# Mixed attention and a SwiGLU feed-forward block on one core: a scheduled kernel rewritten with a hand-written order of 128-query tiles and 512-token groups

## The chip, the cores and the metric

The kernel runs on one core of one Trainium2 chip. The metric is device time in microseconds (us) of one execution; lower is better. A core has five engines that run beside each other, each working through its own queue in order: TensorE (PE in the profile; PEld is its loading of weights), VectorE (DVE), ScalarE (ACT), GpSimd (POOL) and SyncE (SP), which here issues all the DMA transfers. TensorE writes into PSUM, eight banks of 512 fp32 columns on 128 partitions.

## The reference, cut to what matters

Four batches, eight heads, 768 positions, head size 64. Heads 0, 2 and 6 ("retrieval") attend to all earlier positions; the other five ("streaming") attend to the first 4 positions (the sinks) and the last 64. The attention output, 3072 tokens by 512, goes through a SwiGLU feed-forward block of width 1536.

```python
    scores = scale * np.matmul(q, k.transpose(0, 1, 3, 2))
    causal = rel >= 0
    is_sink = pos[None, :] < int(n_sink)
    in_win = (rel >= 0) & (rel < int(window))
    stream_keep = causal & (is_sink | in_win)
    ...
    a = np.exp(scores)
    a = a / (np.sum(a, axis=-1, keepdims=True) + 1e-09)
    return np.matmul(a, v).astype(np.float32)

    g = x @ w_gate
    silu = g * (1.0 / (1.0 + np.exp(-g)))
    val = x @ w_val
    return (silu * val @ w_out).astype(np.float32)
```

## The kernel before

The program is written batch by batch, and a scheduler places its instructions in the engines' queues by priority, so that work of one batch can run among that of another where the queues and buffers allow it.

For a batch, q, k and v are loaded as six blocks of 128 positions each (lines 160, 161, 170; each transfer reads 256-byte runs), cast to half precision on ScalarE (q, line 162) and VectorE (k, line 163; v, line 173), and transposed on TensorE for two heads at a time (line 186), with the results copied out of PSUM by ScalarE (193) and VectorE (197).

Attention goes head by head over three blocks of 256 queries. Scores come transposed, keys on partitions: a matmul of 64 rows by 256 columns for each block of 128 keys (line 230), two blocks to a PSUM bank, then one exponential on ScalarE (235). A retrieval head takes all key blocks up to the queries' end, a streaming head takes three blocks, and its sinks are an extra matmul with 4 keys (210) and exponential (215). GpSimd multiplies the exponentials by a 0/1 mask (240). The value matmuls (249, and 255 for the sinks) take the exponentials as weights and 66 columns of v, one of them ones, so that the row's sum comes out beside the result; VectorE takes its reciprocal (261) and scales (264). When all heads of a batch are done, the six blocks are transposed once more (273) and copied into the feed-forward input xt (278).

The feed-forward block works on 256 tokens at a time: for each of 12 slices of 128 hidden units, four gate matmuls (291) and four value matmuls (296) of 256 columns into one PSUM bank, a tanh on ScalarE (301) and two products on VectorE (303, 308); then for each 128 tokens twelve output-projection matmuls of 512 columns (313), a copy by VectorE (318) and a store (319). The weights are loaded in large pieces through two staging buffers and cast on ScalarE and VectorE (lines 139, 141, 146), written after batch 0's attention.

What sets the order around the change is therefore the scheduler; nothing in the source says which attention instruction stands between which feed-forward matmuls.

## Time and profile before

| | |
|---|---|
| Median of 3 runs | 432.32 us (430.75 to 437.47) |
| Span of the profiled execution | 429.4 us (the page gives no other time of it) |
| TensorE busy | 377.4 us, 88%, 2760 matmuls |
| TensorE weight loads | 234.0 us, 55% |
| VectorE busy | 243.9 us, 57% |
| ScalarE busy | 190.9 us, 44% |
| GpSimd busy | 140.1 us, 33% |
| DMA | 35.06 MB, mean 82 GB/s |
| Granted TensorE clock, mean | 0.880 |

The profile is of one execution. Busy times are those in which an engine was at work on an instruction; matmuls are pipelined, so that the lengths of neighbours overlap and the distance between two starts says more about their cost than a length does. The page cuts the span into 40 slices and gives for each the busy share of each engine and the granted clock; the views below look into it by stretch, by group and by instruction.

### The profile page before, as it was taken

The numbers are of one execution on the slowest core, as the hardware profiler recorded it, in microseconds if no ns is written. First come the engines' busy times: TensorE is split into PE (matmuls) and PEld (weight loads), VectorE is DVE, ScalarE is ACT, GpSimd is POOL, SyncE is SP. The second block draws the span as 40 slices with busy tenths as digits, with TensorE's granted clock in tenths as the row PEclk, the third lists the DMA queues.
The fourth block names the chain that finished last, engine by engine and source line by source line (L and its number), as shares of the span: only waits on it lengthen the run. The fifth ranks groups of instructions, "written<-read, shape, count | busy, mean of one in ns | idle before, by whom it ended". The sixth has DMA issues, their size and how long they took to land.

```text
span 429.4 us, 7362 instructions
## 1 busy us (share of the span) xinstructions
PE 377.4 (88%) x2760; PEld 234.0 (55%) x2760; DVE 243.9 (57%) x754; ACT 190.9 (44%) x401; POOL 140.1 (33%) x117
## 2 busy tenths in 40 slices
PE   0578688999998989899999988899999988899995
PEld 0234334776674534676765543576766544576672
DVE  1253365687674373776765463586765543566763
ACT  3436848553245666233334765233334755122220
POOL 6145496001014676211003775410103786200000
PEclk9999999999999655699999755599999965599999
DMA  9991735977996471311010000000010000001001
GB/s 183 218 358 24 293 100 179 243 143 167 177 207 144 93 153 21 73 26 49 2 51 25 26 0 2 0 2 36 16 50 26 25 2 0 2 2 49 26 24 49
DMA packets 81090, 35.06 MB, mean 82 GB/s; under 512 B 75424, under 2 KB 75424, under 8 KB 81056
## 3 DMA queue, kind: packets, MB, share of 16 engines
q1 hardware_dynamic: 81056, 34.61, 33.6%
q8 instruction: 21, 0.34, 0.3%
q14 instruction: 13, 0.11, 0.1%
HBM read 28.31 MB, written 6.29 MB: 81 GB/s over the span
## 4 chain that ended last, share of the span: by engine, by line
PE 70%; ACT 9%; DVE 9%; issue 4%; POOL 4%; SPq 2%; DMA 1%; ACTq 0%; POOLq 0%
PE gv L291 15%; PE gv L296 13%; PE o_ps L313 13%; PE sc L230 11%; PE av L249 8%; ACT e L235 6%; POOL e L240 4%; PE trp L186 3%; PE xt_ps L273 2%; PE av L255 2%; ACT sig L301 2%; DVE sil L303 2%; DVE hj L308 2%; PE snk L210 2%; SPq L161 1%
## 5 line engine op out<-in xcount | busy, mean ns | idle before, releaser
L240 POOL TENSOR_TENSOR e<-e,cm 128x512 f16<-128x512 f16 (+1 forms) x96 | 132.9, 1391 | 227.1 <-ACT e L235 226.8
L301 ACT ACTIVATE sig<-gv 128x256 f32<-128x256 f32 x144 | 55.2, 383 | 147.1 <-PE gv L296 135.8
L235 ACT ACTIVATE e<-sc 128x512 f16<-128x512 f32 (+1 forms) x172 | 88.2, 546 | 64.0 <-PE sc L230 39.6
L291 PE MATMUL gv<-xt,wg_sb 128*128 128x256 f16 x576 | 91.0, 278 | 1.8 <-DVE hj L308 0.3
L296 PE MATMUL gv<-xt,wv_sb 128*128 128x256 f16 x576 | 90.6, 279 | 0.0
L230 PE MATMUL sc<-qt,ktt 64*128 64x256 f16 x304 | 79.5, 355 | 12.4 <-ACT e L235 10.5
L313 PE MATMUL o_ps<-wo_sb,hj 128*128 128x512 f16 x288 | 82.0, 380 | 1.7 <-DVE o_sb L318 0.8
L303 DVE SCALAR_TENSOR_TENSOR sil<-sig,gv 128x256 f32<-128x256 f32 x144 | 60.5, 420 | 38.9 <-ACT sig L301 38.6
L291 PEld LDWEIGHTS <-wg_sb 128*128 128x128 f16 x576 | 55.4, 100 | 22.4 <-issue 7.0
L249 PE MATMUL av<-vs,e 128*128 128x66 f16 x608 | 56.5, 229 | 11.1 <-POOL e L240 5.2
L249 PEld LDWEIGHTS <-e 128*128 128x128 f16 x608 | 38.0, 117 | 50.0 <-issue 21.2
L308 DVE TENSOR_TENSOR hj<-sil,gv 128x256 f16<-128x256 f32 x144 | 60.4, 420 | 4.7 <-PE o_ps L313 0.3
L296 PEld LDWEIGHTS <-wv_sb 128*128 128x128 f16 x576 | 57.4, 100 | 7.6
L261 DVE RECIPROCAL rc<-av 128x2 f32<-128x2 f32 x96 | 16.2, 169 | 78.4 <-PE av L255 41.4
L264 DVE TENSOR_SCALAR xb<-av,rc 128x64 f16<-128x64 f32 x192 | 45.5, 279 | 2.5
L230 PEld LDWEIGHTS <-ktt 64*128 64x128 f16 x304 | 25.2, 106 | 37.9 <-issue 25.2
L313 PEld LDWEIGHTS <-hj 128*128 128x128 f16 x288 | 27.7, 97 | 21.8 <-DVE hj L308 2.4
L318 DVE COPY o_sb<-o_ps 128x512 f32<-128x512 f32 x24 | 16.6, 692 | 27.6 <-PE o_ps L313 27.5
L273 PE MATMUL xt_ps<-identh,xb 128*128 128x128 f16 x96 | 19.2, 298 | 3.2 <-DVE xb L264 2.3
L255 PE MATMUL av<-vs,es 4*128 4x66 f16 x80 | 17.9, 224 | 0.0
L197 DVE COPY ktt<-trp 128x384 f16<-128x384 f16 x32 | 11.1, 354 | 11.8 <-PE trp L186 11.5
L193 ACT COPY qt<-trp 128x384 f16<-128x384 f16 x32 | 14.8, 477 | 1.9 <-PE sc L230 1.1
(168 smaller groups left out, 195.6 us busy)
## 6 DMA issues: line engine op xcount, KB each, us to landing
qs<-in_q_dram SPq DMA_DIRECT2D x24, 256.0 KB, 4.9
ks<-in_k_dram SPq DMA_DIRECT2D x24, 256.0 KB, 4.8
vraw<-in_v_dram SPq DMA_DIRECT2D x24, 256.0 KB, 4.7
out_dram<-o_sb SPq DMA_DIRECT2D x24, 256.0 KB, 2.0
wstg<-in_moe_w_gate_dram SPq DMA_DIRECT2D x2, 1536.0 KB, 8.8
wstg<-in_moe_w_val_dram SPq DMA_DIRECT2D x2, 1536.0 KB, 6.4
wstg<-in_moe_w_out_dram SPq DMA_DIRECT2D x6, 512.0 KB, 3.4
```

The lines of the kernel that those rows point to most:

```text
L230: nc.tensor.matmul(sc[:, i - g0, :], ktt[hb:hb + 64, kt * 128:(kt + 1) * 128], qt[hb:hb + 64, qsl],)
L235: nc.scalar.activation(out=e[:, g0:g1, :], in_=sc[:, 0:g1 - g0, :], func=AF.Exp, scale=scale,)
L240: nc.gpsimd.tensor_tensor(out=e[:, ms:ms + nm, :], in0=e[:, ms:ms + nm, :], in1=cm[:, cs:cs + nm, :], op=ALU.mult,)
L249: nc.tensor.matmul(av[:, qh, :], e[:, i, qq], v_sb[kt][:, h, :], start=(i == 0), stop=(i == nav - 1),)
L264: nc.vector.tensor_scalar(out=xb[tb][:, h, :], in0=av[:, qh, 0:64], scalar1=rc[:, qh:qh + 1], scalar2=None, op0=ALU.mult,)
L273: nc.tensor.transpose(xt_ps[:, po * 128:(po + 1) * 128], xb[tb][:, 2 * po:2 * po + 2, :].rearrange("p a b -> p (a b)"), identh,)
L291: nc.tensor.matmul(gv[:, 0, :], wg_sb[:, kk, jf * 128:(jf + 1) * 128], xt[:, kk, c0:c0 + NG], start=(kk == 0), stop=(kk == 3),)
L296: nc.tensor.matmul(gv[:, 1, :], wv_sb[:, kk, jf * 128:(jf + 1) * 128], xt[:, kk, c0:c0 + NG], start=(kk == 0), stop=(kk == 3),)
L301: nc.scalar.activation(out=sig, in_=gv[:, 0, :], func=AF.Tanh, scale=0.5)
L303: nc.vector.scalar_tensor_tensor(out=sil, in0=sig, scalar=1.0, op0=ALU.add, in1=gv[:, 0, :], op1=ALU.mult,)
L308: nc.vector.tensor_mul(out=hj, in0=sil, in1=gv[:, 1, :])
L313: nc.tensor.matmul(o_ps, h_sb[jf][:, tt * 128:(tt + 1) * 128], wo_sb[:, jf, :], start=(jf == 0), stop=(jf == NJ - 1),)
```

## The change

The whole kernel is rewritten, with the same inputs and the same outputs. The scheduler is switched off (`tc.manual_schedule()`): each engine's queue holds its instructions in the order of the source.

- Work is cut into 24 tiles of 128 queries, all heads together, and 6 feed-forward groups of 512 tokens (four tiles). The matmuls of gate and value have 512 columns and a PSUM bank each; three banks go round. Scores have one buffer of two banks, values, transposes and the output projection one bank each.
- Attention uses exact blocks of 128 keys by 128 queries: a retrieval head takes i + 1 blocks for tile i, a streaming head one or two; from the third tile of a batch on the second block is a built one (`k2`, `v2`) that holds the sinks and the last 64 positions before the tile, so the separate sink matmuls go. A unit of scores holds up to four blocks for each half of the 64-row pairs (`s` is 0 or 1, partitions 0 to 63 or 64 to 127) and one exponential of up to 1,024 columns.
- Casts of q and k are on VectorE, of v on GpSimd. Weights come in 18 chunks of 512 KB (runs of 1 KB for gate and value, 2 KB for the projection) through five staging buffers; gate chunks are cast on VectorE, the others on GpSimd. Masks are on GpSimd, but for the diagonal blocks of later units on VectorE. Output copies move from VectorE to ScalarE.
- Attention's steps are listed (`tile_items`). The steps up to tile 3's last transpose are issued first. Then each group issues, for each of 12 slices, gate, value and a third of a projection of the group before, and after each of these a share (`beat`) of the attention steps of the tiles that the next group needs. Masks of a step are issued one beat later. The last group has no attention left, and its own projection follows alone.

The core of the diff, added lines (the functions removed are those printed above):

```diff
+    ctx.enter_context(tc.manual_schedule())
...
+    wstage = ctx.enter_context(tc.tile_pool(name="wstage", bufs=5))
+    raw = ctx.enter_context(tc.tile_pool(name="raw", bufs=4))
+    half = ctx.enter_context(tc.tile_pool(name="half", bufs=2))
+    epool = ctx.enter_context(tc.tile_pool(name="epool", bufs=7))
+    hpool = ctx.enter_context(tc.tile_pool(name="hpool", bufs=2 * NJ))
+    ps_gv = ctx.enter_context(tc.tile_pool(name="ps_gv", bufs=3, space=PSUM))
+    ps_o = ctx.enter_context(tc.tile_pool(name="ps_o", bufs=1, space=PSUM))
+    ps_sc = ctx.enter_context(tc.tile_pool(name="ps_sc", bufs=1, space=PSUM))
+    ps_av = ctx.enter_context(tc.tile_pool(name="ps_av", bufs=1, space=PSUM))
+    ps_tr = ctx.enter_context(tc.tile_pool(name="ps_tr", bufs=1, space=PSUM))
...
+    for n in range(2):
+        nc.gpsimd.memset(vt[n][:, :, :, 64:66], 1.0)
+        nc.gpsimd.memset(k2[n], 0.0)
+        nc.gpsimd.memset(v2[n], 0.0)
...
+    worder = [(kd, c) for c in range(NJ // 2) for kd in "gv"] + [("o", c) for c in range(NJ // 2)]
+    wnext = [0, 0]
+    def wstep(n=1):
+        for _ in range(n):
+            if wnext[1] >= len(worder):
+                return
+            while wnext[0] < len(worder) and wnext[0] < wnext[1] + 5:
+                wload(*worder[wnext[0]])
+                wnext[0] += 1
+            wcast(*worder[wnext[1]])
+            wnext[1] += 1
+    def cast(t):
+        b, i = divmod(t, NT)
+        qk, vr = raws.pop(t)
+        hq = half.tile([128, 2, 2, 256], FH, name="hq", tag="hq")
+        for n in range(2):
+            nc.vector.tensor_copy(
+                out=hq[:, n].rearrange("p r (k d) -> p r k d", d=64),
+                in_=qk[:, n].rearrange("p (k r) d -> p r k d", r=2),
             )
+        nc.gpsimd.tensor_copy(out=vt[b % 2][:, i, :, 0:64], in_=vr)
+        halves[t] = hq
+        if t + 4 < TT:
+            load(t + 4)
+    def transposes(t):
+        b, i = divmod(t, NT)
+        hq = halves.pop(t)
+        tr = ps_tr.tile([128, 2, 4, 128], FH, name="tr", tag="tr")
+        for n in range(2):
+            for p in range(4):
+                nc.tensor.transpose(
+                    tr[:, n, p, :], hq[:, n, p // 2, (p % 2) * 128:(p % 2 + 1) * 128], ident)
+        T = qkT[b % 2]
+        nc.vector.tensor_copy(out=T[:, :, :, i * 128:(i + 1) * 128], in_=tr)
+        K2, V, V2 = k2[b % 2], vt[b % 2], v2[b % 2]
+        if i == 0:
+            nc.gpsimd.tensor_copy(
+                out=K2[:, :, :, 0:NSINK],
+                in_=T[:, 1, :, 0:NSINK].unsqueeze(2).to_broadcast([128, 4, 4, NSINK]))
+            nc.gpsimd.tensor_copy(
+                out=V2[0:NSINK].rearrange("p n h d -> p n (h d)"),
+                in_=V[0:NSINK, 0].rearrange("p h d -> p (h d)").unsqueeze(1).to_broadcast(
+                    [NSINK, 4, 8 * 66]))
+        elif i < NT - 1:
+            nc.gpsimd.tensor_copy(
+                out=K2[:, :, i - 1, 64:128], in_=T[:, 1, :, i * 128 + 64:(i + 1) * 128])
+            nc.gpsimd.tensor_copy(out=V2[64:128, i - 1], in_=V[64:128, i])
...
+    def scores(t, u, unit):
+        b, i = divmod(t, NT)
+        T = qkT[b % 2]
+        sc = ps_sc.tile([128, 2, 4, 128], FP, name="sc", tag="sc")
+        e = epool.tile([128, 2, 4, 128], FH, name="e", tag="e")
+        for n in range(4):
+            for s in range(2):
+                if n < len(unit[s]):
+                    h, _, _, kk, vv = unit[s][n]
+                    p = SIDE[h][0]
+                    nc.tensor.matmul(
+                        sc[:, s, n, :], kk,
+                        T[s * 64:s * 64 + 64, 0, p, i * 128:(i + 1) * 128])
+                    av_blocks.setdefault((t, h), []).append((e[:, s, n, :], vv))
+        na, nb = len(unit[0]), len(unit[1])
+        if na == nb:
+            nc.scalar.activation(out=e[:, :, 0:na], in_=sc[:, :, 0:na], func=AF.Exp, scale=scale)
         else:
+            for s, n in ((0, na), (1, nb)):
+                if n:
                     nc.scalar.activation(
+                        out=e[:, s, 0:n], in_=sc[:, s, 0:n], func=AF.Exp, scale=scale)
+        def masks():
+            if i == 0:
+                nc.gpsimd.tensor_tensor(
+                    out=e.rearrange("p s n q -> p (s n) q"),
+                    in0=e.rearrange("p s n q -> p (s n) q"), in1=m0, op=ALU.mult)
+                return
+            if u == 0:
+                ev = e.rearrange("p s (h n) q -> p (s h) (n q)", n=2)
+                nc.gpsimd.tensor_tensor(
+                    out=ev, in0=ev,
+                    in1=m1.rearrange("p n q -> p (n q)").unsqueeze(1).to_broadcast([128, 4, 256]),
+                    op=ALU.mult)
+                return
+            for s in range(2):
+                for n, (h, m, total, _, _) in enumerate(unit[s]):
+                    if not RETR[h]:
+                        if m == 0:
+                            nc.gpsimd.tensor_tensor(
+                                out=e[:, s, n:n + 2], in0=e[:, s, n:n + 2], in1=m1, op=ALU.mult)
+                    elif m == total - 1:
+                        nc.vector.tensor_tensor(
+                            out=e[:, s, n], in0=e[:, s, n], in1=diag, op=ALU.mult)
+        deferred.append(masks)
+    def values(t, odd):
+        if t not in xbs:
+            xbs[t] = xpool.tile([128, 4, 2, 64], FH, name="xb", tag="xb")
+        xb = xbs[t]
+        av = ps_av.tile([128, 4, 66], FP, name="av", tag="av")
+        for n in range(4):
+            bl = av_blocks.pop((t, 2 * n + odd))
+            for m, (ee, vv) in enumerate(bl):
+                nc.tensor.matmul(
+                    av[:, n, 0:65], ee, vv, start=(m == 0), stop=(m == len(bl) - 1))
+        rc = small.tile([128, 4, 1], FP, name="rc", tag="rc")
+        nc.vector.reciprocal(out=rc, in_=av[:, :, 64:65])
+        nc.vector.tensor_tensor(
+            out=xb[:, :, odd, :], in0=av[:, :, 0:64],
+            in1=rc.to_broadcast([128, 4, 64]), op=ALU.mult)
+    def xtranspose(t):
+        g, n = divmod(t, GT)
+        if g not in xts:
+            xts[g] = xtp.tile([128, 4, GT * 128], FH, name="xt", tag="xt")
+        xb = xbs.pop(t)
+        tr = ps_tr.tile([128, 4, 128], FH, name="xtr", tag="tr")
+        for p in range(4):
+            nc.tensor.transpose(tr[:, p, :], xb[:, p].rearrange("p a d -> p (a d)"), ident)
+        nc.vector.tensor_copy(out=xts[g][:, :, n * 128:(n + 1) * 128], in_=tr)
...
+    def tile_items(t):
+        ss = []
+        if t < TT:
+            units = plan_of(t)
+            ss = [(0.3, scores, (t, u, None)) for u in range(len(units))]
+        other = []
+        if t > 0:
+            other.append((0.4, values, (t - 1, 0)))
+        if t + 1 < TT:
+            other.append((0.5, transposes, (t + 1,)))
+        if t < TT:
+            other.append((0.3, values, (t, 1)))
+        if t > 0:
+            other.append((0.25, xtranspose, (t - 1,)))
+        seq = []
+        while ss or other:
+            if ss:
+                seq.append(ss.pop(0))
+            if other:
+                seq.append(other.pop(0))
+        for c, f, a in seq:
+            if f is transposes:
+                add(0.0, cast, a[0] + 1) if a[0] + 1 < TT else None
+            add(c, f, *a)
+            if f is xtranspose:
+                ends[a[0]] = len(items)
...
+    def flush():
+        todo, deferred[:] = deferred[:], []
+        for f in todo:
+            f()
+    def attend(upto):
+        while pos[0] < upto:
+            run(items[pos[0]])
+            pos[0] += 1
+    def gate(g, j):
+        xt = xts[g]
+        ps = ps_gv.tile([128, 512], FP, name="gate", tag="gv")
+        for kk in range(4):
+            nc.tensor.matmul(
+                ps, wg_sb[:, kk, j * 128:(j + 1) * 128], xt[:, kk, :],
+                start=(kk == 0), stop=(kk == 3))
+        sig = ffns.tile([128, 512], FP, name="sig", tag="sig")
+        nc.scalar.activation(out=sig, in_=ps, func=AF.Tanh, scale=0.5)
+        return ps, sig
+    def val(g, j, ps, sig):
+        xt = xts[g]
+        pv = ps_gv.tile([128, 512], FP, name="val", tag="gv")
+        for kk in range(4):
+            nc.tensor.matmul(
+                pv, wv_sb[:, kk, j * 128:(j + 1) * 128], xt[:, kk, :],
+                start=(kk == 0), stop=(kk == 3))
+        sil = ffns.tile([128, 512], FP, name="sil", tag="sil")
+        nc.vector.scalar_tensor_tensor(
+            out=sil, in0=sig, scalar=1.0, op0=ALU.add, in1=ps, op1=ALU.mult)
+        h = hpool.tile([128, 512], FH, name="h", tag="h")
+        nc.vector.scalar_tensor_tensor(
+            out=h, in0=sil, scalar=0.5, op0=ALU.mult, in1=pv, op1=ALU.mult)
+        hs[g, j] = h
+    def outproj(g, n):
+        tt, third = divmod(n, 3)
+        if third == 0:
+            o_open[g] = ps_o.tile([128, DM], FP, name="o_ps", tag="o")
+        o_ps = o_open[g]
+        for j in range(third * 4, third * 4 + 4):
+            nc.tensor.matmul(
+                o_ps, hs[g, j][:, tt * 128:(tt + 1) * 128], wo_sb[:, j, :],
+                start=(j == 0), stop=(j == NJ - 1))
+        if third == 2:
+            o_sb = opool.tile([128, DM], FP, name="o_sb", tag="osb")
+            nc.scalar.copy(out=o_sb, in_=o_ps)
+            r0 = (g * GT + tt) * 128
+            nc.sync.dma_start(out=out[r0:r0 + 128, :], in_=o_sb)
+    cast(0)
+    transposes(0)
+    cast(1)
+    lead = ends[GT - 1]
+    for n in range(lead):
+        attend(n + 1)
+        flush()
+    wstep(4)
+    for g in range(NG):
+        start = pos[0]
+        stop = ends[min(GT * (g + 2), TT) - 1]
+        beats = NJ * (3 if g else 2)
+        done = 0
+        def beat():
+            nonlocal done
+            done += 1
+            flush()
+            attend(start + (stop - start) * done // beats)
+        for j in range(NJ):
+            ps, sig = gate(g, j)
+            beat()
+            val(g, j, ps, sig)
+            beat()
+            if g:
+                outproj(g - 1, j)
+                beat()
+            else:
+                wstep(2)
+    for n in range(NJ):
+        outproj(NG - 1, n)
```

## Rows read from the trace of the kernel before

**Rows 1.** Windows by granted clock: length, busy by engine, PEclk, DMA share, GB/s
```profile
0.00:80.70 80.70, 54.34 (x347) 28.16 (x348) 34.38 (x119) 43.95 (x73) 42.55 (x45) 1.00 0.79 200
80.70:142.10 61.40, 58.72 (x455) 39.52 (x454) 42.12 (x137) 27.10 (x62) 9.46 (x8) 1.00 0.87 174
142.10:179.70 37.60, 33.25 (x228) 17.81 (x228) 20.22 (x72) 21.15 (x44) 22.98 (x17) 0.50 0.36 73
...
346.90:374.20 27.30, 23.78 (x158) 13.18 (x158) 11.41 (x47) 10.58 (x21) 15.11 (x11) 0.50 0.00 1
...
318.00:346.90 28.90, 27.58 (x247) 17.05 (x244) 16.09 (x53) 17.34 (x39) 14.81 (x12) 1.00 0.05 19
```

**Rows 2.** The page's chain that ended last, its shares by line
```profile
PE gv L291 15%; PE gv L296 13%; PE o_ps L313 13%; PE sc L230 11%; PE av L249 8%; ACT e L235 6%; POOL e L240 4%; PE trp L186 3%; PE xt_ps L273 2%; PE av L255 2%; ACT sig L301 2%; DVE sil L303 2%; DVE hj L308 2%; PE snk L210 2%; SPq L161 1%
```

**Rows 3.** Groups of instructions by shape: busy us, mean ns, idle before
```profile
L291 PE MATMUL gv<-xt,wg_sb 128*128 128x256 f16 x576 | 91.0, 278 | 1.8 <-DVE hj L308 0.3
...
L313 PE MATMUL o_ps<-wo_sb,hj 128*128 128x512 f16 x288 | 82.0, 380 | 1.7 <-DVE o_sb L318 0.8 <-DVE hj L308 0.7
...
L235 ACT ACTIVATE e<-sc 128x512 f16<-128x512 f32 x132 | 77.0, 596 | 61.5 <-PE sc L230 37.1 <-PE av L249 21.4 <-POOL e L240 1.7
L240 POOL TENSOR_TENSOR e<-e,cm 128x768 f16<-128x768 f16 x40 | 66.9, 1674 | 31.9 <-ACT e L235 31.7
...
L303 DVE SCALAR_TENSOR_TENSOR sil<-sig,gv 128x256 f32<-128x256 f32 x144 | 60.5, 420 | 38.9 <-ACT sig L301 38.6
...
L318 DVE COPY o_sb<-o_ps 128x512 f32<-128x512 f32 x24 | 16.6, 692 | 27.6 <-PE o_ps L313 27.5
L261 DVE RECIPROCAL rc<-av 128x2 f32<-128x2 f32 x96 | 16.2, 169 | 78.4 <-PE av L255 41.4 <-PE av L249 36.7
L235 ACT ACTIVATE e<-sc 128x256 f16<-128x256 f32 x40 | 15.2, 380 | 2.4 <-PE sc L230 2.4
...
L278 DVE COPY xt<-xt_ps 128x512 f16<-128x512 f16 x24 | 10.0, 422 | 6.1 <-PE xt_ps L273 5.6
...
L163 DVE CAST kh__4341<-ks 128x512 f16<-128x512 f32 x1 | 1.8, 1785 | 0.0
...
L107 POOL MEMSET cm<- 128x1792 f16 x1 | 1.6, 1595 | 0.0
```

**Rows 4.** PE's timeline in a mixed stretch: start us, length, what, count [idle before]
```profile
319.04 0.59 PE L313 MATMUL o_ps<-wo_sb,hj 128*128 128x512 f16 x2
319.57 0.28 PE L230 MATMUL sc<-qt,ktt 64*128 64x256 f16 x1
319.78 0.61 PE L291 MATMUL gv<-xt,wg_sb 128*128 128x256 f16 x4
...
330.81 2.75 PE L313 MATMUL o_ps<-wo_sb,hj 128*128 128x512 f16 x12
333.40 0.28 PE L249 MATMUL av<-vs,e 128*128 128x66 f16 x4
...
334.75 0.65 PE L230 MATMUL sc<-qt,ktt 64*128 64x256 f16 x4 [0.30 <-ACT e L235]
...
341.30 0.52 PE L249 MATMUL av<-vs,e 128*128 128x66 f16 x12
341.76 0.50 PE L230 MATMUL sc<-qt,ktt 64*128 64x256 f16 x3
```

**Rows 5.** Windows, columns as in rows 1: two stretches of loading
```profile
0.00:10.00 10.00, 0.86 (x3) 0.32 (x3) 1.16 (x4) 3.28 (x5) 7.22 (x21) 1.00 1.01 180
20.00:30.00 10.00, 7.40 (x46) 3.44 (x46) 6.05 (x19) 4.40 (x10) 4.80 (x4) 1.00 1.15 346
```

**Rows 6.** Timeline of all engines: a cast of 128x512 without company
```profile
12.87 0.42 DVE L163 CAST kh__164<-ks 128x512 f16<-128x512 f32 x1
```

**Rows 7.** PE's last stretch in the timeline: a projection that waited for a copy
```profile
422.85 2.75 PE L313 MATMUL o_ps<-wo_sb,hj 128*128 128x512 f16 x12 [0.78 <-DVE o_sb L318]
```

More of the change, by code (lines that the diff above doesn't have):

```diff
@@ L12 @@
 ALU = mybir.AluOpType
+PSUM = bass.MemoryType.PSUM
 @with_exitstack
@@ L81 @@
[L81 to L86 removed]
+    PAIRS = [(0, 2), (4, 6), (1, 3), (5, 7)]
+    SIDE = {h: (p, s) for p, pr in enumerate(PAIRS) for s, h in enumerate(pr)}
@@ L87 @@
+    for t in range(4):
+        load(t)
+    ident = const.tile([128, 128], FH, name="ident")
+    nc.gpsimd.memset(ident, 0.0)
     nc.gpsimd.affine_select(
[L88 removed]
+        out=ident, in_=ident, compare_op=ALU.not_equal, fill=1.0,
         base=0, pattern=[[-1, 128]], channel_multiplier=1,
     )
[L92 to L105 removed]
@@ new lines, in keep @@
+    def keep(ap, base, qstep, kstep):
+        nc.gpsimd.affine_select(
+            out=ap, in_=ap, compare_op=ALU.is_ge, fill=0.0, base=base,
+            pattern=[[qstep, 128]], channel_multiplier=kstep,
+        )
+    m0 = const.tile([128, 8, 128], FH, name="m0")
+    m1 = const.tile([128, 2, 128], FH, name="m1")
+    diag = const.tile([128, 128], FH, name="diag")
+    band0 = const.tile([128, 128], FH, name="band0")
+    nc.gpsimd.memset(diag, 1.0)
+    keep(diag, 0, 1, -1)
+    nc.gpsimd.memset(band0, 1.0)
@@ new lines @@
+    keep(band0, WIN - 1, -1, 1)
+    nc.gpsimd.memset(band0[0:NSINK, :], 1.0)
+    keep(band0, 0, 1, -1)
+    nc.gpsimd.memset(m1, 1.0)
+    keep(m1[:, 0, :], WIN - 1, -1, 1)
+    keep(m1[:, 0, :], 0, 1, -1)
+    keep(m1[:, 1, :], WIN - 1 - 128, -1, 1)
+    nc.gpsimd.memset(m1[0:64, 1, :], 0.0)
+    nc.gpsimd.memset(m1[0:NSINK, 1, :], 1.0)
+    for n_, src in enumerate((band0, band0, band0, diag, band0, band0, diag, diag)):
+        nc.gpsimd.tensor_copy(out=m0[:, n_, :], in_=src)
+    qkT = [const.tile([128, 2, 4, S], FH, name=f"qkT{n}") for n in range(2)]
@@ new lines @@
+    k2 = [const.tile([128, 4, 4, 128], FH, name=f"k2_{n}") for n in range(2)]
+    vt = [const.tile([128, NT, 8, 66], FH, name=f"vt{n}") for n in range(2)]
+    v2 = [const.tile([128, 4, 8, 66], FH, name=f"v2_{n}") for n in range(2)]
+    for n in range(2):
+        nc.gpsimd.memset(vt[n][:, :, :, 64:66], 1.0)
+        nc.gpsimd.memset(k2[n], 0.0)
+        nc.gpsimd.memset(v2[n], 0.0)
+    wg_sb = const.tile([128, 4, DFF], FH, name="wg_sb")
+    wv_sb = const.tile([128, 4, DFF], FH, name="wv_sb")
@@ new lines, in keys_of, with plain @@
+    def keys_of(t, h):
+        b, i = divmod(t, NT)
+        p, s = SIDE[h]
+        rows = slice(s * 64, s * 64 + 64)
+        T, K2, V, V2 = qkT[b % 2], k2[b % 2], vt[b % 2], v2[b % 2]
+        def plain(kt):
+            return T[rows, 1, p, kt * 128:(kt + 1) * 128], V[:, kt, h, 0:65]
+        if RETR[h]:
+            return [plain(kt) for kt in range(i + 1)]
+        if i == 0:
+            return [plain(0)]
+        if i == 1:
+            return [plain(1), plain(0)]
+        return [plain(i), (K2[rows, p, i - 2, :], V2[:, i - 2, h, 0:65])]
@@ new lines, with add @@
+    xts = {}
+    def xtranspose(t):
[7 more added lines that the diff above has]
+        nc.vector.tensor_copy(out=xts[g][:, :, n * 128:(n + 1) * 128], in_=tr)
+    items = []
+    ends = {}
+    def add(cost, f, *a):
+        items.append((cost, f, a))
@@ new lines, in plan_of, with run @@
+    def plan_of(t):
+        i = t % NT
+        a, b_ = (4, 4) if i == 0 else (7 + i, 6 + 2 * i)
+        return range((max(a, b_) + 3) // 4)
+    for t in range(TT + 1):
+        tile_items(t)
+    plans = {}
+    def run(item):
+        _, f, a = item
+        if f is scores:
+            t, u, _ = a
+            if t not in plans:
+                plans[t] = plan(t)
+            f(t, u, plans[t][u])
+        else:
+            f(*a)
+    pos = [0]
+    def flush():
+        todo, deferred[:] = deferred[:], []
+        for f in todo:
+            f()
```

322 lines of the change are left out of this document (65 added, 257 removed).

## Prediction

> **What bounds the kernel now.** I read the page's slices first, then windows cut at the changes of granted clock, then the chain, the groups by shape and the timeline of TensorE. The chain is mostly TensorE, spread over the two feed-forward matmuls, the output projection, and attention's scores and values [rows 2]. The windows say why that is not simply a full engine [rows 1]. The kernel alternates: 61.4 us with TensorE at full clock, then 37.6 us at 0.50, the 1.2 GHz level. The stretch 241.1 to 278.7 repeats the one shown, and 346.9 to 374.2 is the last. In the slow stretches VectorE and GpSimd are busy a little over half the time each and no feed-forward work is ready, since it waits for the batch's attention. The first 80.7 us are attention of batch 0 during loading; the clock column shows 1.00 there, but no change of clock is recorded before 80.7. Attention standing alone so takes 80.7 + 2 x 37.6 + 27.3 = 183.2 us of the 429.4 us span. The rest, 246 us, is feed-forward work at the full clock with some attention mixed in by the scheduler. The span is that of one execution; the median of the runs lies 2.9 us above it, and I add that at the end.
>
> **Feed-forward work.** It neither shrinks nor grows: before, 2 x 576 matmuls of 256 columns and 288 of 512 [rows 3]; after, 864 of 512, which is the same 442,368 columns. Twelve matmuls of 512 columns take 2.59 us from start to start [rows 4], 0.216 us each, so 864 x 0.216 = 186.6 us. This is the floor that the new order tries to reach, with attention's instructions between.
>
> **Attention on TensorE.** It covers 128-query tiles with exact blocks: 8, 16, 19, 22, 25 and 28 blocks for the six tiles of a batch, 118 in all, 19.7 a tile. Each block is one score matmul of 128 columns and one value matmul of 65. Scores drop from 304 + 40 matmuls of 256 columns to 472 of 128, values from 688 to 472; transposes stay 288. At the full clock value matmuls start 0.038 us apart (twelve in 0.46) and scores of 256 columns 0.11 us apart, by the difference between lengths of three and of one [rows 4]. Half of that, 0.055, is my price for 128 columns, and for a transpose. Bounds for a score are 0.038 (the value matmul, nearest in columns) and 0.11 (if columns did not matter); I take the half since feed-forward time goes with columns. Per tile: 19.7 x (0.055 + 0.038) + 12 x 0.055 = 2.5 us.
>
> Entering and leaving costs too. A score matmul started 0.10 us later behind a projection than two projections take, and the next matmul came 0.21 us after it rather than 0.11 [rows 4]: 0.20 us for a lone visit. A tile makes 6.8 visits (2.83 score units, two value groups, two transposes). At 0.17 us as a mean of such visits that is 1.2 us; at the 0.30 us that a score waited for an exponential [rows 4] on every visit it is 2.0 us more. So a tile costs 3.7 us, between 2.8 and 6.8. Tiles 0 to 3 are done before the feed-forward work; 20 tiles remain: 74 us, bounds 57 to 136.
>
> The Trainium skill's page "TensorEngine Tiling (Array Packing)", section Key Properties, says that different row tiles of the array can load weights and multiply in parallel. The new scores alternate between the two halves of 64 rows; no row here shows two halves at once. By that rule a score would cost half, and the sum would fall by some 11 us.
>
> **The other engines in a group.** Per group of 512 tokens and four tiles TensorE has 144 x 0.216 + 4 x 3.7 = 46 us. VectorE: 256 columns from PSUM take 0.420 and 512 take 0.692 [rows 3], so 24 such operations are 16.6 us. A tile adds two casts at 0.42 [rows 6], an eviction of 1,024 half-precision columns at about 0.7 (0.422 for 512, rows 3), the copy of x at 0.42, two reciprocals at 0.17, two scalings of 256 columns at 0.42 and three diagonal masks, estimated at 0.17 each: 3.7 us. VectorE's group is then 31 us. ScalarE: 0.38 us for 256 and 0.596 for 512 columns give 1.03 for 1,024; 12 tanh, 11.3 exponentials and four output copies are 21 us. GpSimd: a mask of 768 columns takes 1.67 [rows 3], so 1,024 take 2.2; with the mask of head 4, the cast of v and the copies for the streaming keys about 5 us a tile, 20 us a group. All are under 46 us, so I cost their work at nothing; if the cover fails they show as waits of TensorE, which now works in program order. The three buffers of the gate and value sums give VectorE about one projection and one visit of slack.
>
> **The start.** Loads of q, k and v run at 180 to 200 GB/s [rows 1, 5], 0.79 MB a tile, 3.9 us. GpSimd first fills masks and two sets of constant tiles; at 1.6 us for 1,792 columns [rows 3] the four zero fills of some 2,080 columns take 7.4 us, and mask work kept GpSimd busy for 7.2 of the first 10 us before [rows 5], so its first cast of v starts near 14 us and its first mask ends near 20. The value matmuls queue behind that, and all of TensorE behind them. Then twelve score units follow one another through one score buffer: 8 score matmuls at the slow clock, twice 0.055 each, 0.88, an exponential 1.03, hand-overs 0.2, some 2.1 us each, 25 us. That gives 46 us. Bounds: 36 (seven tiles of loads and one chunk of weights) and 60 (the pace of batch 0 before, some 12 us a tile). Weights move behind the tile loads in SyncE's queue: their first chunk is issued once tile 6 is cast, near 38 us, and lands about when it is needed.
>
> **The first group** is fed by loads. From about 40 us there are 9.4 MB of weights, at about 300 GB/s between 200 and 346 [rows 1, 5], and three more tiles, 2.4 MB at 200: 43 us, to 83. Casts of weights sit in the queues of VectorE and GpSimd in program order, so later masks and products stand behind chunks that have not landed; they are all issued by the seventh of twelve steps. The last five steps then take 15 us, to about 98, where TensorE alone would need 46 + 96 x 0.216 + 15 = 82. Some of that is absorbed in slack; I take 12 us of delay, between 0 and 20.
>
> **Joints and tail.** Each of the five next groups begins right behind the last transpose of x, its copy of 0.42 and a VectorE operation of 0.69 ahead of it [rows 3]: 1.4 us each, 7. At the end three projections wait for the copy of the one before, 0.78 us [rows 7], and from the last matmul to the end of the span it is 3.8 us as before (425.6 to 429.4): 6.
>
> **Sum.** 46 + 186.6 + 74 + 12 + 7 + 6 = 331.6 us of span; with 2.9 it is 334.5, say 335 us.
>
> **Rivals.** A: VectorE becomes the bound through GpSimd. A cast of k took 0.42 us alone [rows 6] and 1.79 in a stretch where GpSimd was masking [rows 3]. GpSimd is to be busy 20 us of 46, and five VectorE operations a tile are of the exposed sort. With 1.1 us more each (half a mask), 5.5 us a tile, VectorE's group is 53 us against 46; over five groups 35 us: 370 us. The Trainium skill's page "SBUF — State Buffer", section Who interferes with whom, gives the rule: copies in a two-port mode, and operations with two SBUF inputs, exclude a GpSimd operation that reads SBUF for the whole instruction; the two rows just named agree. Against it stands that the feed-forward products have one input in PSUM and kept their 0.420 mean.
>
> B: the start is as slow as batch 0 was and the first group waits in full: 60 instead of 46 and 20 instead of 12, 357 us.
>
> C: the written order doesn't hide. Each visit stands for its own exponential, mask or copy; with 0.5 us for 137 visits, 335 + 68 = 403 us. It would pass the old time at 0.71 us a visit. For it: the order is fixed, one buffer each serves scores, values and transposes. Against it: two visits with their feed-forward matmuls between last some 2.5 us, more than the exponential's 1.03.
>
> D, the slower side: TensorE loses the full clock in the mixture. At 1.2 GHz each of the 864 matmuls costs double, up to 187 us more, and attention some 40: about 560 us. It passes the old time when just under half of the feed-forward matmuls run slow. Against it: from 318 us to 346.9 the same mixture of scores, values, transposes and feed-forward work ran at 1.00, with TensorE busy 27.6 of 28.9 us [rows 1].
>
> **How the numbers follow.** Forecast 0.74, A 0.08, B 0.06, C 0.07, D 0.05. The range runs from 310 (a score at its low price and little delay at the start) to 380, which takes in A and B and leaves out most of C and D. Runs of the old kernel differ by 1.6%, so about 2% is what can be told from no change. Faster by over 2% (under 423.7): forecast, A, B and part of C, 0.91; within 2%: 0.02, of C; slower: 0.07, D and the rest of C.
>
> **What would show it.** Right: one early stretch of about 46 us, a granted clock at 1.00 to the end from soon after the first gate matmul, TensorE's idle time small and ended by several engines, groups of 45 to 49 us, the last without attention near 32. Wrong: casts and diagonal masks of VectorE far above 0.5 us (A); gate matmuls ended by weight casts past 95 us (B); value matmuls ended by GpSimd's masks in every tile (C); feed-forward matmuls 0.43 us apart (D). A score at 0.03 or at 0.11 us would move the sum by 11 or 22 us.

## The result and the profile after

The changed kernel takes 319.32 us (median of 4 runs, 316.9 to 320.44), against 434.89 us for the kernel before in runs on the same chip: a ratio of 0.741, interval [0.7355, 0.7457]. Two of the four runs of the kernel before took 437.5 us, in a slower state of the chip, and the ratio leaves them out. The forecast was 335 us, its range 310 to 380. The profiled execution took 320.0 us, with a span of 318.3.

The page of the kernel after: its busy times, two rows of its 40 slices, and the chain by line, which answers to [rows 2].

```profile
PE 263.1 (83%) x2096; PEld 133.0 (42%) x2096; DVE 212.0 (67%) x402; ACT 116.3 (37%) x177; POOL 132.5 (42%) x152
...
PE   0035761976886999998999999999899998999984
...
PEclk9999999997998999999999999999999999999999
...
PE o_ps L436 20%; PE gate L406 18%; PE val L417 17%; DVE hq L192 8%; PE sc L266 6%; ACT e L272 3%; PE av L314 3%; PE tr L207 2%; DMA wst<-in_moe_w_val_dram 2%; DMA wst<-in_moe_w_out_dram 2%; DMA wst<-in_moe_w_gate_dram 2%; DVE h L424 2%; PE xtr L331 1%; DVE qkT L210 1%; DVE e L299 1%
```

The slow stretches of [rows 1] are gone: the granted clock stays at nine tenths or more but for two slices, at 0.7 and 0.8. From the fourteenth slice on TensorE is busy for eight or nine tenths or more up to the last slice; the slack that is left lies in the first third and at the very end. In the chain, attention's scores and values fell from 19% to 9%, and a new entry stands fourth: VectorE's casts of q and k (L192), 8%.

Windows of the kernel after, cut at the first gate matmul of each group and at 299.8, behind the last value matmul. Columns as in [rows 1]. The two groups left out took 41.3 and 41.5 us.

```profile
0.00:56.44 56.44, 20.93 (x228) 15.01 (x228) 37.64 (x55) 13.29 (x17) 37.61 (x58) 1.00 0.75 175
56.44:100.30 43.86, 34.60 (x293) 17.12 (x294) 39.18 (x70) 15.52 (x23) 31.88 (x31) 0.96 0.86 261
100.30:145.20 44.90, 43.35 (x366) 21.55 (x366) 31.53 (x65) 19.73 (x30) 17.49 (x17) 0.96 0.33 81
145.20:186.70 41.50, 40.98 (x344) 20.35 (x344) 30.96 (x68) 19.37 (x31) 17.09 (x18) 1.00 0.44 110
...
269.50:299.80 30.30, 30.27 (x141) 13.72 (x141) 15.21 (x23) 8.93 (x15) 0.00 (x0) 1.00 0.09 35
299.80:318.30 18.50, 11.97 (x53) 4.91 (x51) 1.29 (x2) 2.93 (x5) 0.00 (x0) 1.00 0.19 71
```

A full group takes 41.4 us. The last group, which has no attention beside it, has issued 140 matmuls of 512 columns in 30.3 us: 0.216 us each, the forecast's price. So four tiles of attention cost a group only some 10 us, and TensorE is busy for 41.0 of the 41.5 us of the full group shown. VectorE at 31 us and ScalarE at 19 us stay under TensorE, as forecast (31 and 21).

TensorE's timeline in a full group shows what a visit to attention costs. Columns as in [rows 4].

```profile
151.78 1.03 PE L406 MATMUL gate<-xt,wg_sb 128*128 128x512 f16 x4
152.65 0.40 PE L314 MATMUL av<-vt,e 128*128 128x65 f16 x8
152.89 1.03 PE L417 MATMUL val<-xt,wv_sb 128*128 128x512 f16 x4
153.75 0.39 PE L331 MATMUL xtr<-ident,xb 128*128 128x128 f16 x4
153.97 1.03 PE L436 MATMUL o_ps<-wo_sb,h 128*128 128x512 f16 x4
154.93 0.23 PE L266 MATMUL sc<-qkT 64*128 64x128 f16 x2
155.00 0.22 PE L266 MATMUL sc<-qkT,k 64*128 64x128 f16 x2
155.06 0.22 PE L266 MATMUL sc<-qkT 64*128 64x128 f16 x2
155.11 0.22 PE L266 MATMUL sc<-qkT,k 64*128 64x128 f16 x2
155.26 1.04 PE L406 MATMUL gate<-xt,wg_sb 128*128 128x512 f16 x4
```

Read the starts. Four matmuls of 512 columns take 0.86 to 0.87 us, and the value matmuls come right behind them: eight take 0.24, 0.030 each, and leaving them is free. Four transposes take 0.22, 0.055 each, and are free to enter and leave too. Only the scores cost a change: they start 0.96 us after the projection instead of 0.86, and their eight take 0.33 although a pair starts every 0.06. That is 0.23 for the scores and about 0.19 for the visit, half of it on entering and half on leaving. No wait stands in these lines: here the exponentials and masks are hidden.

### The profile page after: what moved, and what is told of

Its sections match the earlier page's. It is cut to its first block, busy times and chain, and to the rows that moved or that the text cites. A ratio compares the mean times of both kernels' runs of the same rounds, so it can differ in the third digit from the quotient of the medians.

```text
span 318.3 us, 5386 instructions
## 1 busy us (share of the span) xinstructions
PE 263.1 (83%) x2096; PEld 133.0 (42%) x2096; DVE 212.0 (67%) x402; ACT 116.3 (37%) x177; POOL 132.5 (42%) x152
## 4 chain that ended last, share of the span: by engine, by line
PE 67%; DVE 14%; DMA 6%; POOL 5%; ACT 4%; SPq 1%; issue 1%; DVEq 0%; ACTq 0%; POOLq 0%
PE o_ps L436 20%; PE gate L406 18%; PE val L417 17%; DVE hq L192 8%; PE sc L266 6%; ACT e L272 3%; PE av L314 3%; PE tr L207 2%; DMA wst<-in_moe_w_val_dram 2%; DMA wst<-in_moe_w_out_dram 2%; DMA wst<-in_moe_w_gate_dram 2%; DVE h L424 2%; PE xtr L331 1%; DVE qkT L210 1%; DVE e L299 1%
## 5 line engine op out<-in xcount | busy, mean ns | idle before, releaser
L406 PE MATMUL gate<-xt,wg_sb 128*128 128x512 f16 x288 | 75.5, 385 | 12.6 <-DVE wg_sb L161 7.0
L421 DVE SCALAR_TENSOR_TENSOR sil<-sig,gate 128x512 f32<-128x512 f32 x72 | 49.2, 684 | 45.7 <-ACT sig L410 45.6
L410 ACT ACTIVATE sig<-gate 128x512 f32<-128x512 f32 x72 | 43.0, 597 | 100.2 <-PE gate L406 100.2
L417 PE MATMUL val<-xt,wv_sb 128*128 128x512 f16 x288 | 76.5, 389 | 1.8 <-DVE sil L421 1.8
L436 PE MATMUL o_ps<-wo_sb,h 128*128 128x512 f16 x288 | 73.4, 382 | 2.8 <-ACT o_sb L441 2.8
L287 POOL TENSOR_TENSOR e<-e,m 128x1024 f16<-128x1024 f16 x20 | 42.6, 2132 | 66.3 <-ACT e L272 66.3
L272 ACT ACTIVATE e<-sc 128x1024 f16<-128x1024 f32 x48 | 49.1, 1022 | 53.3 <-PE sc L266 49.1
L424 DVE SCALAR_TENSOR_TENSOR h<-sil,val 128x512 f16<-128x512 f32 x72 | 49.5, 688 | 8.4 <-PE val L417 0.7
L192 DVE CAST hq<-rawqk 128x512 f16<-128x512 f32 x48 | 45.2, 981 | 4.4 <-DMA rawqk<-in_q_dram 4.0
L417 PEld LDWEIGHTS <-wv_sb 128*128 128x128 f16 x288 | 25.8, 99 | 30.5 <-issue 3.3
```

The lines of the kernel that those rows point to most:

```text
L192: nc.vector.tensor_copy(out=hq[:, n].rearrange("p r (k d) -> p r k d", d=64), in_=qk[:, n].rearrange("p (k r) d -> p r k d", r=2),)
L272: nc.scalar.activation(out=e[:, :, 0:na], in_=sc[:, :, 0:na], func=AF.Exp, scale=scale)
L287: nc.gpsimd.tensor_tensor(out=ev, in0=ev, in1=m1.rearrange("p n q -> p (n q)").unsqueeze(1).to_broadcast([128, 4, 256]), op=ALU.mult)
L406: nc.tensor.matmul(ps, wg_sb[:, kk, j * 128:(j + 1) * 128], xt[:, kk, :], start=(kk == 0), stop=(kk == 3))
L410: nc.scalar.activation(out=sig, in_=ps, func=AF.Tanh, scale=0.5)
L417: nc.tensor.matmul(pv, wv_sb[:, kk, j * 128:(j + 1) * 128], xt[:, kk, :], start=(kk == 0), stop=(kk == 3))
```

## Where the start went

All engines, early in the kernel after:

```profile
4.87 0.75 POOL L121 COPY m<-band 128x128 f16<-128x128 f16 x3
4.91 9.51 DVE L192 CAST hq<-rawqk 128x512 f16<-128x512 f32 x1 [0.39 <-DMA rawqk<-in_k_dram]
...
12.29 1.85 POOL L132 MEMSET v<- 128x2112 f16 x1
14.09 0.79 POOL L196 CAST vt<-rawv 128x512 f16<-128x512 f32 x1
...
14.47 0.61 PE L207 MATMUL tr<-ident,hq 128*128 128x128 f16 x4 [9.29 <-DVE hq L192]
...
21.02 0.40 PE L314 MATMUL av<-vt,e 128*128 128x65 f16 x4 [3.57 <-POOL e L281]
```

One cast on VectorE, 0.42 us when alone [rows 6], stayed unfinished for 9.51 us while GpSimd ran its copies and fills one behind the other, and TensorE's first transposes of k waited 9.29 us for it. The first value matmuls came at 21.02, behind GpSimd's first mask. The end of the start, from the timeline of all engines (SPq is SyncE's queue of transfers):

```profile
48.80 0.61 PE L331 MATMUL xtr<-ident,xb 128*128 128x128 f16 x4
...
50.61 1.08 SPq L150 DMA_DIRECT2D wst<-in_moe_w_gate_dram  x1
...
55.69 0.69 DVE L161 CAST wg_sb<-wst 128x1024 f16<-128x1024 f32 x1 [5.38 <-DMA wst<-in_moe_w_gate_dram]
...
56.44 1.89 PE L406 MATMUL gate<-xt,wg_sb 128*128 128x512 f16 x4 [7.03 <-DVE wg_sb L161]
```

TensorE's part of tile 3 is done near 49.4 us. Then TensorE waits 7.03 us for the cast of the first gate weights, and the cast waits for a load that was issued only at 50.61. Groups by shape in the kernel after:

```profile
L192 DVE CAST hq<-rawqk 128x512 f16<-128x512 f32 x48 | 45.2, 981 | 4.4 <-DMA rawqk<-in_q_dram 4.0 <-DMA rawqk<-in_k_dram 0.4
...
L299 DVE TENSOR_TENSOR e<-e,diag 128x128 f16<-128x128 f16 x60 | 19.0, 346 | 9.6 <-ACT e L272 8.2 <-ACT e L276 1.3
```

The casts mean 0.98 us and the diagonal masks 0.35, where the forecast had 0.42 and 0.17. For the casts that is rival A's mechanism; what it was worth had to be tried. The masks' 0.17 was an estimate, so their 0.35 alone doesn't show it.

## The experiments

Each is an edit of the changed kernel. Ratios are to the kernel before, run on the same chip (its medians were 431.8 to 433.2 us).

**The order undone: attention of the next tiles in one piece, between groups.**

```diff
             flush()
-            attend(start + (stop - start) * done // beats)
+        for n in range(start, stop):
+            attend(n + 1)
+            flush()
```

> All attention steps of the next group's four tiles are issued ahead of a group's feed-forward matmuls instead of between them; the work is the same. Theory (the interleaving makes the gain): a tile alone took some 6.5 us in the start of the changed kernel (29.2 to 48.8 us for three), against 2.6 us between feed-forward matmuls; 20 tiles cost 78 us more, less some 10 us of waiting for weights in the first group: 385 to 396 us, with the granted clock falling to 0.50 in each stretch of attention. Rival (fewer and cheaper matmuls make the gain, the order little): under 335 us.

Measured: 391.57 us, ratio 0.904 [0.8998, 0.9085], inside the theory's range. Windows of this kernel: a feed-forward stretch, and the attention alone behind it.

```profile
133.80:165.50 31.70, 31.70 (x144) 14.14 (x143) 15.95 (x25) 8.92 (x15) 0.63 (x2) 0.96 0.18 50
165.50:192.90 27.40, 17.09 (x204) 12.45 (x203) 19.25 (x44) 11.46 (x16) 17.17 (x18) 0.59 0.41 96
```

Its timeline of TensorE in the second stretch:

```profile
167.84 0.40 PE L266 MATMUL sc<-qkT 64*128 64x128 f16 x8 [1.04 <-ACT e L272]
...
172.64 0.59 PE L331 MATMUL xtr<-ident,xb 128*128 128x128 f16 x4 [2.09 <-DVE qkT L210]
```

Four tiles alone take 27.4 us, 6.9 a tile, with the clock down to 0.59, mostly its 1.2 GHz level, and TensorE waiting over and over (two of the waits are shown); between feed-forward matmuls they take about 10. TensorE stands idle for 10.3 of the 27.4 us; what the low clock adds to that isn't separated, so the worth of the order is that of cover and clock together. The rewriting without the order gives 433 to 392 us; the order gives the other 72. The rival, that the order matters little, falls.

**Coarser: attention only at every third matmul group (every second in the first group).**

```diff
-            attend(start + (stop - start) * done // beats)
+            if done % (3 if g else 2) == 0:
+                attend(start + (stop - start) * done // beats)
```

> Attention steps are issued once a slice of 12, some three at a time, instead of after each of gate, value and projection. Theory (a score unit must have one or two blocks of feed-forward matmuls between it and its exponential's user): in a batch of three steps two score units stand close, and the second waits some 1.3 us for the exponential of the first, once a tile or more: 335 to 350 us. Rival (one stretch of cover a slice is enough, the queues absorb the rest): under 325 us.

Measured: 330.35 us, ratio 0.763 [0.7578, 0.7687], 11 us more: under the theory's range and over the rival's. TensorE's waits in this kernel (us in total, times, longest):

```profile
PE xtr L331 <- DVE qkT L210: 10.6, 6, 2.7
...
PE sc L266 <- ACT e L272: 4.1, 8, 0.8
PE av L314 <- POOL e L287: 4.1, 3, 3.0
```

The same rows of the changed kernel:

```profile
PE xtr L331 <- DVE qkT L210: 7.0, 5, 1.9
PE gate L406 <- DVE xt L332: 5.6, 5, 2.2
...
PE sc L266 <- ACT e L272: 2.4, 6, 0.8
...
PE av L314 <- POOL e L287: 1.4, 3, 0.7
```

Steps crowded into one place wait for each other: 8 us more in these three rows. Rival C's mechanism exists, at a small size; the fine spread is what keeps it away.

**The halves of the array, in another order of issue.**

```diff
-        for n in range(4):
-            for s in range(2):
+        for s in range(2):
+            for n in range(4):
```

> Score matmuls of a unit go through the lower 64 rows first and then the upper, instead of alternating. Theory (two halves of the array work at once): pairs now start 0.003 and 0.056 us apart by turns, so scores cost 0.028 each; in turn they would cost 0.056, 393 of them beside the feed-forward work, 11 us more: 327 to 332 us, and starts 0.056 apart. Rival (the short distance between starts is only how a queue shows): starts as before and the same time within 1 per cent.

Measured: 319.69 us, ratio 0.738 [0.7334, 0.7432]: no change, and starts in pairs as before. That is what the rival stated, and the time alone gives the theory no support. As an undoing of the parallel halves the edit failed, and its timeline of TensorE says why:

```profile
155.26 0.24 PE L266 MATMUL sc<-qkT 64*128 64x128 f16 x2
155.33 0.23 PE L266 MATMUL sc<-qkT,k 64*128 64x128 f16 x2
...
```

Now all four scores of one half are issued first, and among them plain and built blocks (k) alternate. One stream would show single plain and built ones in turn. The starts come in pairs of one kind instead, one from each half, a pair every 0.06 us: the halves run as two streams even when one half's matmuls are all queued ahead of the other's. So the edit doesn't take the overlap away. What a score costs, which is where theory and rival differ, had to be measured in another way.

**Each score matmul issued twice** (the second repeats the first into the same place).

```diff
-                    nc.tensor.matmul(
+                    for _ in range(2):
+                        nc.tensor.matmul(
```

> Every score matmul is issued twice, the second over the same output, to price it; starts in the half-by-half kernel ran in two streams by half whatever the order of issue. Theory (the two halves of 64 rows work side by side, 0.028 us a score): 393 more scores beside the feed-forward work cost 11 us, those of the start some 2: 329 to 334 us. Rival (a score has the price of its 128 columns, 0.056): 340 us or more. Third (scores are hidden by other waits): under 323 us.

Measured: 329.89 us, ratio 0.764 [0.76, 0.768], as the theory said. The window of a full group of this kernel, which answers to the 41.50 us of 145.2 to 186.7:

```profile
148.90:192.90 44.00, 43.51 (x425) 22.87 (x425) 30.93 (x68) 19.75 (x31) 17.07 (x18) 1.00 0.42 105
```

81 recorded matmuls more in 2.5 us: 0.031 us a score, not 0.055. With that the rival of the experiment before, that the short distance is only how a queue shows, falls too.

**Casts of q and k on ScalarE.**

```diff
-            nc.vector.tensor_copy(
+            nc.scalar.copy(
```

> The casts of q and k move from VectorE to ScalarE. Theory (VectorE's casts are held by GpSimd: the cast of the first k took 9.51 us while GpSimd filled its constants, and the mean is 0.98 against 0.42 alone): tile 0's keys come 8 us earlier, each later tile of the start loses 1 to 1.5 us of waiting for a cast: 305 to 311 us, first gate matmul near 48 us. Rival (GpSimd's own queue sets the start, its setup ends at 14.1 us and its mask at 21 whatever VectorE does): first gate matmul no earlier than 54 us, 316 us or more.

Measured: 309.25 us, ratio 0.715 [0.7112, 0.7195], 10 us less, as the theory said (its start is 1.6 us longer than stated). Its first value and first gate matmuls and, from the view of groups, its casts:

```profile
19.28 0.40 PE L314 MATMUL av<-vt,e 128*128 128x65 f16 x4 [9.71 <-POOL e L281]
...
49.57 1.04 PE L406 MATMUL gate<-xt,wg_sb 128*128 128x512 f16 x2 [6.73 <-DVE wg_sb L161]
```
```profile
L192 ACT CAST hq<-rawqk 128x512 f16<-128x512 f32 x48 | 27.5, 621 | 5.4 <-DMA rawqk<-in_q_dram 3.4 <-DMA rawqk<-in_k_dram 2.0
```

The casts take their steady 0.62 us there. The start is 6.9 us shorter and the first two groups some 3.5. The full groups stay at 41.3 to 41.5 us although VectorE lost up to eight casts a group: in them it wasn't the bound, so rival A is out as a bound and stands as a cost of the start. The rival has a part of the truth: without one held cast the first value matmul comes only 1.7 us earlier, since GpSimd's own queue of fills is as long as before. And 6.73 us of waiting for weights are still there.

**Zero fills of k2 and v2 on VectorE instead of GpSimd.**

```diff
-        nc.gpsimd.memset(k2[n], 0.0)
-        nc.gpsimd.memset(v2[n], 0.0)
+        nc.vector.memset(k2[n], 0.0)
+        nc.vector.memset(v2[n], 0.0)
```

> Only the four zero fills of the tiles for the streaming keys and values, 7.3 us of GpSimd's setup, move to VectorE; the casts stay there. Theory (GpSimd's setup is the first wait of the start, by its own queue and by holding VectorE's casts): its first cast of v starts near 7 instead of 14 us, the first value matmuls near 14 instead of 21, the first gate matmul 6 to 8 us earlier: 310 to 314 us. Rival (VectorE's casts or the loads set the start anyway): first gate matmul after 54 us, 316 us or more.

Measured: 313.22 us, ratio 0.720 [0.712, 0.7281], as the theory said. Its timelines of VectorE and of TensorE:

```profile
1.09 0.91 DVE L131 MEMSET k<- 128x1024 uint32 x1 [1.09 <-PEq L494]
...
5.21 0.78 DVE L192 CAST hq<-rawqk 128x512 f16<-128x512 f32 x2
...
13.52 0.40 PE L314 MATMUL av<-vt,e 128*128 128x65 f16 x4 [4.02 <-POOL e L281]
...
49.44 1.03 PE L406 MATMUL gate<-xt,wg_sb 128*128 128x512 f16 x2 [7.39 <-DVE wg_sb L161]
```

The fills take half as long on VectorE, the two casts of tile 0 behind them take 0.78 us together, and GpSimd's first mask starts at 11.4 us instead of 18.9. The first gate matmul starts at 49.44. Two things had made the start long, and each of the last two edits takes away one. Up to the first value matmul GpSimd's queue sets the time: 21.02 us in the changed kernel, 19.28 with no cast held, 13.52 with the fills gone. From there to the wait for weights it is the casts in VectorE's queue, most of them held: 28.4 us, 23.6 with the casts on ScalarE, 28.5 with only the fills moved. So the cast held for 9.51 us, the most striking line of the start, cost some 1.7 us; the casts behind it cost 4.8.

**The first five weight chunks loaded ahead of the start's last tiles.**

```diff
+    for n in range(5):
+        wload(*worder[n])
+    wnext[0] = 5
```

> The first five chunks of weights are issued on SyncE's queue right after the loads of tiles 0 to 3 instead of behind the loads of tiles 4 to 10. Theory (the first gate waits for a load that stands behind others in one queue): the 7 us before the first gate matmul go, tiles 4 and on land up to 9 us later but mostly before their casts, and the first group waits some 5 us less: first gate matmul near 50 us, 305 to 312 us. Rival (the loads as a whole limit the first 100 us, so their order only moves the wait): first gate earlier but first group longer by as much, 316 us or more.

Measured: 313.24 us, ratio 0.727 [0.723, 0.73], between the two. The first gate matmul of this kernel:

```profile
50.62 0.61 PE L410 MATMUL gate<-xt,wg_sb 128*128 128x512 f16 x1 [2.69 <-DVE wg_sb L161]
```

The wait falls from 7.03 to 2.69 us. The other 1.5 us of the earlier start are not this edit's: the kernel of the next experiment, whose start isn't edited, has its first gate matmul 1.6 us earlier too, and in the profiled executions of both, other casts were held than in the changed kernel's. 2.69 us remain since the cast itself is issued only behind tile 3.

**Buffers in the tail: the last group's projections use the three banks of gate and value.**

```diff
-            o_open[g] = ps_o.tile([128, DM], FP, name="o_ps", tag="o")
+            if g == NG - 1:
+                o_open[g] = ps_gv.tile([128, DM], FP, name="o_ps", tag="gv")
+            else:
+                o_open[g] = ps_o.tile([128, DM], FP, name="o_ps", tag="o")
```

> The last group's projections take the three PSUM buffers of gate and value, free by then, instead of the single one. Theory (each projection of the tail waits for the copy of the one before): the four gaps of 1.05 us between projections become 0.22, 3.3 us less: 315 to 317 us. Rival (the end of the span is set by copies and stores): no change, 318 to 320 us.

Measured: 314.79 us (6 runs), ratio 0.729 [0.7256, 0.732], 0.2 us below the theory's range. TensorE's end, in the changed kernel and then its first gate matmul and its end in this one:

```profile
301.45 2.75 PE L436 MATMUL o_ps<-wo_sb,h 128*128 128x512 f16 x12 [0.67 <-ACT o_sb L441]
304.87 2.75 PE L436 MATMUL o_ps<-wo_sb,h 128*128 128x512 f16 x12 [0.67 <-ACT o_sb L441]
```
```profile
54.84 1.89 PE L406 MATMUL gate<-xt,wg_sb 128*128 128x512 f16 x4 [6.92 <-DVE wg_sb L161]
...
297.90 11.39 PE L439 MATMUL o_ps<-wo_sb,h 128*128 128x512 f16 x52
```

Twelve matmuls, a wait for the copy, twelve more: with one bank the projections took 3.42 us each; with three they run through. The tail is 3.4 us shorter, as stated. The rest of the 4.5 us gained can't come from the tail: the start of the profiled execution was 1.6 us shorter as well.

**Those three together** (casts on ScalarE, weights early, tail buffers).

> Casts of q and k on ScalarE, the first weights early, and the tail's buffers, all three. Theory (three separate waits in the start, the first group and the tail): the gains add, 9 + 9 + 3: 294 to 301 us, first gate matmul near 43 us. Rival (they are one wait, of GpSimd's queue in the start or of the loads): 303 us or more.

Measured: 299.97 us, ratio 0.695 [0.6919, 0.6979], as the theory said. The first gate matmul starts at 45.0 us, the tail is 15.0. The longest of TensorE's waits in the start is now for GpSimd's first mask, 10.0 us.

**All of it**: the three, the zero fills on VectorE, and the first four weight casts issued among the last steps of the start instead of behind them:

```diff
     for n in range(lead):
         attend(n + 1)
         flush()
-    wstep(4)
+        if lead - n in (8, 6, 4, 2):
+            wstep(1)
```

> The three changes together, with the zero fills on VectorE and the first four casts of weights issued among the last steps of the start. Theory (the start still waits 10 us for GpSimd's first mask and 2.2 us for the first cast of weights): 5 to 8 us less than the three together: 291 to 295 us. Rival (loads now limit the start, 0.79 MB a tile and 2.6 MB of weights ahead of tile 4): 298 us or more.

Measured: 297.25 us (296.82 to 298.85), ratio 0.685 [0.6792, 0.6917], between the two. Windows of the start and of the first group:

```profile
0.00:41.70 41.70, 21.16 (x227) 15.06 (x228) 23.20 (x46) 20.92 (x31) 31.21 (x56) 1.00 1.02 253
41.70:83.00 41.30, 33.81 (x293) 17.06 (x293) 33.62 (x61) 19.63 (x31) 28.19 (x29) 1.00 0.90 261
```

The DMA share is 1.02 of the start and 0.90 of the first group. Transfers fill both, which is likely why the mended queues bring less together (22 us) than one by one (27); no run tests that. This kernel is 22 us under the changed kernel; if the transfers are the limit, fewer or longer ones come next, which I did not try.

## Why the prediction was right, step by step

| Term, us | Forecast | Measured in the profiled execution |
|---|---|---|
| Start | 46 | 56.4 |
| Feed-forward, 864 matmuls | 186.6 | 186.6 (864 at the measured 0.216) |
| Attention of 20 tiles | 74 | 48 |
| First groups' delay | 12 | 14 |
| Joints | 7 | 5.6 |
| Tail | 6 | 7.3 |
| Sum | 331.6 | 317.9 (span 318.3) |

The measured terms: attention is (41.4 - 144 x 0.216 - 0.7 for a joint) / 4 = 2.4 us a tile from the full groups. The first group is 43.9 - 96 x 0.216 - 4 x 2.4 - 2.2 for its joint = 11.4 over, the second 2.6. Joints are the five waits for xt. The tail is 18.5 less 52 x 0.216. Delay and tail are what is left of their windows, so that the sum closes is no test of them. The median lies 1.0 us above the span, not 2.9.

The mechanism was right: attention went between feed-forward matmuls, the clock stayed up, and TensorE's own work set the time. Against the old clock pattern this shows in the first experiment, where attention alone pulls the clock to 0.59 in the same kernel. Two terms were mis-sized, and they partly cancelled. That the time fell inside the range is in part luck: with attention alone put right the forecast would have been 309 us, below the range's 310, and the measured 2.4 us a tile lie below the forecast's own lower bound of 2.8.

**Attention, 26 us too dear.** The step "Half of that, 0.055, is my price for 128 columns" took one stream of scores; two streams make it 0.028 by the timeline and 0.031 by the doubled scores, 0.5 us a tile less. The step that put 0.17 us on each of 6.8 visits was wrong for four of them: only the 2.8 score visits cost (0.19), 0.6 us a tile less. Value matmuls at 0.030 instead of 0.038 give 0.15. Together 2.3 to 2.4 us a tile. The Trainium skill's page "TensorEngine Tiling (Array Packing)", section Key Properties, states both: tiles of the array load and multiply in parallel, and a change of tiling mode drains the engine. The trace agrees on both, with 0.06 us a pair and about 0.10 us on each side of a score visit; the page gives no price. The forecast named the first and the row to check it by, and kept the dearer price since no row showed two halves at once.

**The start, 10 us too short.** The first value matmul came about when the forecast had it, at 21.02 us against near 20, and for its reason, GpSimd's queue: its first cast of v began at 14.09, as forecast. TensorE's part of tile 3 ended at 49.4 instead of 46, and the first gate matmul waited 7.03 us more.

The step that failed for the 7 us is that the first weights land "about when it is needed": the forecast has their load issued once tile 6 is cast, near 38 us. In the written order tile 6's cast is among the last steps before tile 3 is done; it ended at 48.0, the loads of tile 10 followed it in the queue, and the weights' load went out at 50.61. Held casts are not the reason, since the wait is 6.73 us with the casts on ScalarE and 7.39 with the fills moved, and 2.69 with the loads put ahead.

The other 3.4 us go with VectorE's casts, held by rival A's mechanism, which I had priced at half a mask each and in the groups only: twelve units at 2.1 us were to take 25 us, and they took 28.4, or 23.6 with the casts on ScalarE. The Trainium skill's page "SBUF — State Buffer", section Who interferes with whom, has an exclusive lock on a port pair, with the other engine blocked until the holder is done. The trace goes further: the 9.51 us of the held cast are those of a run of fourteen GpSimd instructions, none over 1.9 us.

**The small terms.** A joint's two terms in the forecast, 0.42 and 0.69, add to 1.1 us and not to its 1.4; the five waits are 0.5 to 2.2. In the tail four projections waited, not three.

**The rivals.** A was no bound (full groups unmoved when the casts left VectorE), but cost up to 10 us at the start and in the first two groups. B came half: a start of 56.4 against its 60, a delay of 14 against its 20. C showed 11 us when the steps were crowded, and little in the kernel as written: later masks of GpSimd and the exponentials cost TensorE 3.8 us in all by the two rows of its waits, VectorE's diagonal masks 1.9 more. D did not come.

**The other marks.** Groups were forecast at 45 to 49 us and took 41.3 to 41.5, with 44.9 for the second; the last without attention took 30.3 to its last projection of the group before, where I had said near 32. Gate matmuls waiting for weight casts past 95 us did not occur: that row has one wait, the 7.03 us at 56.4.

## What to carry to other kernels

Where one kind of work lets TensorE's clock fall and another keeps it up, write the order by hand, and spread the first in pieces of a fraction of a microsecond between the second: here the spreading was worth 72 us, and a third as many places cost 11 of them back. Then read the two ends by themselves: the first 100 us and the last 18 held nearly all of the 22 us that the later edits took off. Look there for setup work in GpSimd's queue ahead of the first mask, for casts on VectorE beside a busy GpSimd, for weight loads queued behind data that isn't needed sooner, and for a single PSUM bank that has to be copied out before the next sum.

## What the runs showed of the hardware

- A VectorE cast from fp32 in SBUF to half precision, 0.42 us alone, was held for 9.51 us by GpSimd instructions that followed each other without a break; with the four fills off GpSimd, this cast and its neighbour took 0.78 us together, and on ScalarE such casts took 0.61 to 0.63 us each. Which cast is caught differs between kernels that are alike there: with the tail's buffers alone changed, the first two took 0.43 and 0.47 us and the next four 13.58 us together.
- Score matmuls on the two 64-row halves run as two streams whatever their order in the queue: a pair every 0.06 us, with one half's four all issued ahead of the other's.
- Passing between 128-row matmuls of different kinds and sizes costs nothing (next starts 0.030 and 0.055 us on); passing to the 64-row scores and back costs about 0.10 us each way.
- The page's clock column reads 1.00 for the first 56 us, yet value matmuls start 0.054 us apart there (eight from 47.76 to 48.14) against 0.030 in a full group. At the start the pace says more than the column.
